# Two spacer tiles of 72 and 0 floats in place of 56 and 16: the experts' rows and activations move up by 64 bytes

## The chip, the cores and the metric

One core of a Trainium2 chip runs the whole program. The metric is the device time in microseconds (us) of one execution; three executions of the kernel before are known, and one more was taken with the profiler.

## The reference

The input is `x` of 8 x 2496 x 256 floats. A Fourier layer comes first: an FFT along the sequence, a complex 256 x 256 matrix, a soft threshold, the inverse FFT. Its result, 19968 rows of 256, goes through a mixture of 8 experts, of which each row takes one:

```python
logits = x @ w_gate + modality_bias[modality_id]
e_idx = np.argmax(logits, axis=1)
...
for e in range(E):
    mask = e_idx == e
    h = np.maximum(x[mask] @ w1[e], 0.0)
    out[mask] = gate_w[mask, None] * (h @ w2[e])
```

`w1[e]` is 256 x 1024, `w2[e]` 1024 x 256, all float32.

## The kernel before

The first part (classes `Attn`, `Route` and `SplitWeights`) does the Fourier layer in eight batches, routes each batch's rows, scatters them by expert into a DRAM buffer `xs`, and writes the experts' weights, split into a high and a low part, to DRAM. It ends near 639 us. The second part (class `Experts`) is the one whose tiles the change moves.

`Experts.run` goes through 40 tiles, 38 of 512 rows and 2 of 256 rows, each of one expert. Two sets of weight tiles take turns, `i % 2`: `wb[0]` lies at the far end of SBUF, `wb[1]` is made last in `Experts.pools`. For a tile, `load_x` reads the rows, `prep` transposes them on VectorE, `sums` forms four block sums, and `parts` splits every block into a rounded part `xh` (ScalarE, L937) and a rest `xl` (GpSimd mostly, L938). Then there are two layers on TensorE, each in two groups `grp`:

- `layer1` (L958) makes seven products of six matmuls each. The weights `w` are the stationary operand, loaded by LDWEIGHTS; `xh` or `xl`, 256 columns, is the moving operand. ScalarE copies three of the products to `v1`, `v2`, `v3` (L972), VectorE adds them (L967), ScalarE makes the rounded activations `hh` (L963) and VectorE the rest `hl` (L964).
- `layer2` (L1020) takes `hh` or `hl` as the stationary operand and 256 columns of `w2` as the moving one. ScalarE multiplies by the gate weight (L1037), and GpSimd scatters the rows to the output (L1053).

`run` interleaves the two layers by a fixed string, one product of `layer1` (six matmuls) and half a block of `layer2` (six matmuls) in turn, so that TensorE sees x x x x x x y y y y y y and so on; five small tiles of 32 rows are put in between (`tiny`). No planner and no due time is at work on the engines in this part: the order of each engine is the order in which the code records it.

Where tiles lie in SBUF is set by the order in which `Experts.pools` opens its pools, each behind the one before:

```python
self.x = pool("mx", 2)
self.tr = pool("mtr", 1)
self.cp = pool("mc", 1)
...
pad("mq0", PADS[0])
self.xp = pool("mxs", 1)
self.s = pool("ms", 1)
self.h = [pool("mh0", 1), pool("mh1", 1)]
pad("mq1", PADS[1])
self.wb.append(self.sets(ctx, 1))
```

`pad` makes a pool with one tile of so many floats per partition, which nothing reads or writes, and nothing at all for 0. Every tile behind `mq0` is a multiple of 1024 bytes long per partition (1024 for `xh` and `xl`, 2048 for `v`, 8192 for `hh`, `hl`, `w2`, `w3`, 14336 for `w0`, `w1`), so all tiles of a pool share one residue of 1024 bytes; pieces of a tile lie at that residue or 512 behind it.

One place of the first part is of use below. `Attn.pivot` (L424) has `pv` as the moving operand, whose first half lies at residue 448, and a piece of the tile `z` as the stationary one. The pieces of successive `j` begin 480 bytes apart (three steps of 160), so their residues run through multiples of 32 while the shape of the matmul stays; in batch 5 the first half's piece lies at 512 for j = 8, at 448 for j = 10 and at 384 for j = 12.

Of the kernel before, what the change touches and what calls it, by code (L numbers as in the profile page):

```python
# [41 lines left out]
SLOTS = 5  # L42
MORE = 16
EARLY = (6 * SEQ - 8 * (TP - 1)) // TP + 1 - E
PADS = (56, 16)
W1 = 2 * 2 * 7 * 128
W2 = 2 * 4 * 256
RAW = (2, 4, 6, 8, 10)
# [748 lines left out]
class Experts:  # L797
# [13 lines left out]
    def pools(self, ctx):  # L811
# [10 lines left out]
                                pattern=[[-1, 128]], channel_multiplier=1)  # L822
# [6 lines that stand above are left out]
# [750 lines left out]
```

## Time and profile before

| | |
|---|---|
| runs of the kernel before | 1508.08, 1508.33, 1509.77 us; median 1508.33 |
| the profiled execution | 1507.88 us, of which its span 1506.1 us |
| TensorE busy | 1430.0 us, 95% of the span |
| VectorE, ScalarE, GpSimd busy | 976.8, 799.9 and 804.7 us (65%, 53%, 53%) |
| mean granted TensorE clock | 0.982 |
| experts' matmuls | 7032, from 638.9 to 1493.8 us |

The span goes from the first to the last instruction of the profiled execution, and the 1.8 us that its time has over it lie around it. "Busy" is the time in which an engine has an instruction in work; matmuls overlap, so a TensorE that is busy all the time may still take longer or shorter steps from one matmul to the next. That step is read from the starts in the timeline.

### The profile page before, as it was taken

To read this page: it belongs to the slowest core of one execution; us is meant where nothing else is said; L and a number is where in the kernel's file an instruction comes from. 1 tells how busy PE (TensorE), PEld (TensorE's weight loads), DVE (VectorE), ACT (ScalarE), POOL (GpSimd) and SP (SyncE) were. 2 spreads that over 40 slices of the span, in tenths; PEclk is the share of its full clock that TensorE was granted. 3 is DMA by queue.
4 is the path that set the end of the run, shared out by engine and by line. 5 is a ranking of instruction groups with operands and counts; after the bars stand their busy time and mean duration, and the time that the engine had idled before them with its cause. 6 is when DMAs were issued, how large, how long until landed. Compare 5 with 4: busy or idle time off the path is not lost. (4 is left out here: it accounts for less than half of the span.)

```text
span 1506.1 us, 33730 instructions
## 1 busy us (share of the span) xinstructions
PE 1430.0 (95%) x11988; PEld 1366.3 (91%) x11988; DVE 976.8 (65%) x1882; ACT 799.9 (53%) x1715; POOL 804.7 (53%) x946
## 2 busy tenths in 40 slices
PE   8899898989898968989999999999999999999996
PEld 5789898979897968989999999999999999999995
DVE  4577776767686867577776566566656656665651
ACT  3456565656565434655455555555555555555542
POOL 2464767676767576734446844344434444444442
PEclk9999999999999989999999999999999999999998
DMA  8978787888787666851222359324212851582192
GB/s 269 284 231 255 241 273 243 273 247 268 251 268 232 220 206 197 297 175 36 54 57 60 98 149 360 78 50 102 70 36 51 285 187 42 166 305 55 40 353 75
DMA packets 222325, 268.85 MB, mean 179 GB/s; under 512 B 120784, under 2 KB 173771, under 8 KB 216901
## 3 DMA queue, kind: packets, MB, share of 16 engines
q1 hardware_dynamic: 202611, 223.67, 48.6%
q0 software_dynamic: 19408, 42.83, 8.9%
q8 instruction: 97, 1.59, 0.5%
q14 instruction: 79, 0.65, 0.1%
q10 hardware_dynamic: 130, 0.12, 0.0%
HBM read 326.99 MB, written 113.36 MB: 292 GB/s over the span
## 5 line engine op out<-in xcount | busy, mean ns | idle before, releaser
L1020 PE MATMUL y<-w,hh 128*128 128x256 f32 x2496 | 460.5, 279 | 0.0
L1020 PEld LDWEIGHTS y<-w,hh 128*128 128x128 f32 x2496 | 380.6, 189 | 3.7 <-issue 3.7
L1020 PE MATMUL y<-w,hl 128*128 128x256 f32 x1248 | 347.4, 278 | 2.2 <-DVE hl L964 2.0
L958 PE MATMUL X<-xh,w 128*128 128x256 f32 x1248 | 272.6, 282 | 6.9 <-ACT v L972 6.6
L1053 POOL DMA_INDIRECT out<-o,ix x156 | 154.9, 993 | 194.2 <-ACT o L1037 159.6
L1020 PEld LDWEIGHTS y<-w,hl 128*128 128x128 f32 x1248 | 234.2, 188 | 3.8 <-DVE hl L964 3.8
L958 PEld LDWEIGHTS X<-xh,w 128*128 128x128 f32 x1248 | 212.9, 188 | 12.4 <-ACT v L972 10.4
L938 POOL TENSOR_TENSOR xl<-tr,xh 128x256 fp32r<-128x256 f32 x118 | 88.4, 750 | 177.7 <-ACT xh L937 177.1
L964 DVE SCALAR_TENSOR_TENSOR hl<-Y,hh 128x512 fp32r<-128x512 f32 x156 | 107.8, 691 | 109.9 <-ACT hh L963 109.9
L958 PE MATMUL X<-xl,w 128*128 128x256 f32 x624 | 174.7, 280 | 1.1 <-POOL xl L938 1.1
L963 ACT ACTIVATE hh<-Y 128x512 fp32r<-128x512 f32 x156 | 93.3, 598 | 131.4 <-DVE Y L967 125.2
L424 PE MATMUL pv<-pv,z 128*120 128x136 f32 x704 | 118.8, 299 | 36.2 <-DVE z L414 35.3
L938 POOL TENSOR_TENSOR xl<-xt,xh 128x256 fp32r<-128x256 f32 x150 | 110.2, 746 | 79.9 <-ACT xh L937 75.0
L972 ACT COPY v<-X 128x512 f32<-128x512 f32 x228 | 133.6, 586 | 18.5 <-PE X L958 10.8
L424 PEld LDWEIGHTS pv<-pv,z 128*120 128x120 f32 x704 | 104.0, 200 | 39.1 <-issue 36.3
L958 PE MATMUL Z<-xh,w 128*128 128x256 f32 x608 | 132.3, 282 | 0.0
L382 PE MATMUL mx<-wmix,Xh 128*128 128x256 f32 x640 | 116.6, 305 | 6.6 <-DVE mx L372 5.6
L958 PEld LDWEIGHTS X<-xl,w 128*128 128x128 f32 x624 | 117.2, 188 | 1.6 <-POOL xl L938 1.6
L598 POOL DMA_INDIRECT xs<-x1b,si x88 | 89.5, 1017 | 49.5 <-DVE pl L430 21.2
L598 POOL DMA_INDIRECT xs<-x,si x88 | 89.4, 1016 | 42.4 <-issue 16.0
L967 DVE TENSOR_TENSOR Y<-Z,v 128x512 f32<-128x512 f32 x76 | 53.0, 698 | 88.8 <-ACT v L972 88.7
L429 ACT CAST ph<-pv 120x264 fp32r<-120x264 f32 x176 | 66.9, 381 | 80.5 <-PE pv L424 70.6
(259 smaller groups left out, 3484.0 us busy)
## 6 DMA issues: line engine op xcount, KB each, us to landing
w<-wsp SPq DMA_DIRECT2D x80, 1792.0 KB
w<-wsp SPq DMA_DIRECT2D x80, 1024.0 KB
a<-scr SPq DMA_DIRECT2D x160, 128.0 KB
x<-in_x SPq DMA_DIRECT2D x38, 512.0 KB
xt<-xs SPq DMA_DIRECT2D x152, 128.0 KB
scr<-ev SPq DMA_DIRECT2D x35, 480.0 KB
wsp<-wh SPq DMA_DIRECT2D x64, 256.0 KB
x<-in_moe_w SPq DMA_DIRECT2D x40, 256.0 KB
```

The costliest lines, as they stand in the source:

```text
L382: nc.tensor.matmul(mx[:, i, :], t[:, c, 1 - i, :], self.w[:, i, c, lo, :], start=False, stop=n == 5, skip_group_check=True)
L424: nc.tensor.matmul(ps[:PK, c * 128:c * 128 + D // 2 + E], self.z[:, o:o + 3, :, :].rearrange("p n k r -> p (n k r)"), self.pv[:, c, :], st ...
L429: nc.scalar.copy(ph, ps[:PK, :GC])
L598: i = self.nc.gpsimd.indirect_dma_start(out=self.xs, out_offset=bass.IndirectOffsetOnAxis(ap=si[:, k:k + 1], axis=0), in_=rows, in_offset= ...
L938: (nc.gpsimd if i or j in (0, 1, 6) else nc.vector).tensor_sub(sq(xl), v, sq(xh))
L958: nc.tensor.matmul(ps[:, u, :], w1[:, lo, u, blk, :], x, start=start and u == k == 0, stop=k == 2, skip_group_check=True)
L963: nc.scalar.activation(hh[:, par::2, o], v, AF.Relu)
L964: nc.vector.scalar_tensor_tensor(hl[:, par::2, o], v, 0.0, hh[:, par::2, o], ALU.max, ALU.subtract)
L967: nc.vector.tensor_add(out, a, b)
L972: nc.scalar.copy(v, ps)
L1020: nc.tensor.matmul(ps, h[:, q, o], w2[:, lo, q, :], start=grp == s % 2 == q == k == 0, stop=grp == 1 and q == 3 and k == 2, skip_group_che ...
L1053: ins = self.nc.gpsimd.indirect_dma_start(out=self.out, out_offset=bass.IndirectOffsetOnAxis(ap=ix, axis=0), in_=o, in_offset=None, bounds ...
```

## The change

```diff
-PADS = (56, 16)
+PADS = (72, 0)
```

`mq0` grows from 224 to 288 bytes per partition, and `mq1` (64 bytes) is no longer made. Every instruction of the built program stays, in the same order on all five engines and with the same waits. Of all tiles in SBUF, PSUM and DRAM only those of `mxs`, `ms`, `mh0` and `mh1` get other addresses, 64 bytes higher. By the built program's table of tiles, bytes within a partition and their residue of 1024:

```
tiles                     before            after
tr (mtr)                  61088,  672       61088,  672
xh0 .. xl6 (mxs)          69536,  928       69600,  992
v1, v2, v3 (ms)           83872,  928       83936,  992
hh, hl of group 0 (mh0)   90016,  928       90080,  992
hh, hl of group 1 (mh1)  106400,  928      106464,  992
w0 .. w3, set 1 (mw1)    122848,  992      122848,  992
w0 .. w3, set 0 (mw0)    184288,  992      184288,  992
```

So while TensorE streams `xh` and loads the next piece of `w` beside it, the two lay 64 bytes apart by residue (or 64 and 512), with the moving operand below; in the second layer, with `w2` moving and `hh` loaded, 64 apart with the moving one above. After the change both distances are 0 (or 512). At the seams between the layers, where `w2` streams and `w` is loaded, or `xh` streams and `hh` is loaded, the distance was 0 (or 512) before and stays so.

## Rows read from the trace of the kernel before

**Rows 1.** The page: busy time, share of the span, instructions of each engine.

```profile
PE 1430.0 (95%) x11988; PEld 1366.3 (91%) x11988; DVE 976.8 (65%) x1882; ACT 799.9 (53%) x1715; POOL 804.7 (53%) x946
```

**Rows 2.** Stretches: length, busy (instructions) of each engine, clock, DMA share, GB/s.

```profile
850.00:900.00 50.00, 50.00 (x432) 50.00 (x432) 30.55 (x50) 28.58 (x62) 28.96 (x37) 1.00 0.46 117
...
1000.00:1100.00 100.00, 100.00 (x872) 98.39 (x871) 61.01 (x96) 56.59 (x123) 45.01 (x59) 1.00 0.30 73
...
1300.00:1400.00 100.00, 100.00 (x867) 97.86 (x866) 60.36 (x95) 56.00 (x122) 46.01 (x62) 1.00 0.61 190
```

**Rows 3.** Waits of TensorE's weight loads, 850 to 1390 us: total us, times, longest.

```profile
PEld y L1020 <- issue: 3.3, 8, 0.4
PEld X L958 <- ACT hh L963: 1.6, 4, 0.4
```

**Rows 4.** Groups of instructions: the experts' matmuls; busy us, mean ns of one | idle before.

```profile
L1020 PE MATMUL y<-w,hh 128*128 128x256 f32 x2496 | 460.5, 279 | 0.0
L1020 PE MATMUL y<-w,hl 128*128 128x256 f32 x1248 | 347.4, 278 | 2.2 <-DVE hl L964 2.0
L958 PE MATMUL X<-xh,w 128*128 128x256 f32 x1248 | 272.6, 282 | 6.9 <-ACT v L972 6.6
L958 PE MATMUL X<-xl,w 128*128 128x256 f32 x624 | 174.7, 280 | 1.1 <-POOL xl L938 1.1
L958 PE MATMUL Z<-xh,w 128*128 128x256 f32 x608 | 132.3, 282 | 0.0
L958 PE MATMUL Z<-xl,w 128*128 128x256 f32 x304 | 85.1, 280 | 0.0
L958 PE MATMUL Y<-xh,w 128*128 128x256 f32 x336 | 73.0, 281 | 0.0
L958 PE MATMUL Y<-xl,w 128*128 128x256 f32 x168 | 47.1, 280 | 0.0
```

**Rows 5.** Timeline of PE, 1160.33 to 1164.55 us: start us, us, what.

```profile
1160.33 0.28 PE L958 MATMUL X<-xh,w 128*128 128x256 f32 x1
...
1160.92 0.28 PE L958 MATMUL X<-xh,w 128*128 128x256 f32 x1
1161.05 0.40 PE L1020 MATMUL y<-w,hh 128*128 128x256 f32 x2
...
1161.75 0.28 PE L958 MATMUL Y<-xh,w 128*128 128x256 f32 x1
...
1162.33 0.28 PE L958 MATMUL Y<-xh,w 128*128 128x256 f32 x1
1162.44 0.39 PE L1020 MATMUL y<-w,hh 128*128 128x256 f32 x2
...
1163.13 0.28 PE L958 MATMUL X<-xh,w 128*128 128x256 f32 x1
...
1164.55 0.28 PE L958 MATMUL Z<-xh,w 128*128 128x256 f32 x1
```

**Rows 6.** Timeline of PE, batch 5, j = 5, 8, 10, 12 and 21 of the pivot.

```profile
477.56 0.63 PE L424 MATMUL pv<-pv,z 128*120 128x136 f32 x4
...
480.06 0.63 PE L424 MATMUL pv<-pv,z 128*120 128x136 f32 x4
...
482.41 0.63 PE L424 MATMUL pv<-pv,z 128*120 128x136 f32 x4
...
484.78 0.63 PE L424 MATMUL pv<-pv,z 128*120 128x136 f32 x4
...
493.31 0.63 PE L424 MATMUL pv<-pv,z 128*120 128x136 f32 x4
```

**Rows 7.** Groups of instructions: those of the other engines that touch moved tiles.

```profile
L938 POOL TENSOR_TENSOR xl<-xt,xh 128x256 fp32r<-128x256 f32 x150 | 110.2, 746 | 79.9 <-ACT xh L937 75.0 <-PE Z L958 3.3
L964 DVE SCALAR_TENSOR_TENSOR hl<-Y,hh 128x512 fp32r<-128x512 f32 x156 | 107.8, 691 | 109.9 <-ACT hh L963 109.9
L963 ACT ACTIVATE hh<-Y 128x512 fp32r<-128x512 f32 x156 | 93.3, 598 | 131.4 <-DVE Y L967 125.2 <-PE Y L958 6.2
```

**Rows 8.** The chain that ended last: start us, us, what.

```profile
1497.60 0.98 POOL out L1053
```

## The prediction

> **What bounds the kernel now.** I read the page first, then a table of stretches, then the waits, and last the timeline of TensorE. On the page TensorE is busy for 95% of the span, the other engines for 53 to 65% [rows 1]. The change touches no tile that is used before the experts begin, so only the part from 639 us on matters. In that part's steady stretch TensorE is busy all the time: 50.00 of 50.00 us, 100.00 of 100.00 us, at a granted clock of 1.00, the higher of the two levels, 2.4 GHz [rows 2]. VectorE is busy for about 61 of 100 us, ScalarE for 56, GpSimd for 45 [rows 2]. In the 540 us from 850 to 1390 the largest waits of TensorE's weight loads come to 3.3 us in 8 times and 1.6 us in 4 times [rows 3]. So nothing but TensorE's own step, from the start of one matmul to the start of the next, sets the length of the stage. The end hangs on it too: the last scatter starts at 1497.60 us [rows 8], some 4 us behind the last of the experts' matmuls.
>
> That step is not one number. In the timeline, a group of six `layer1` and six `layer2` matmuls takes from 1160.33 to 1161.75, so 1.42 us; the next takes to 1163.13, so 1.38 us; the one after that to 1164.55, so 1.42 us again [rows 5]. Per matmul that is 118 ns and 115 ns. The shapes are the same, the clock is full, and no wait stands between. Slow and fast groups alternate. The two kinds of group have the same distances between their operands' addresses, so the distance alone doesn't choose the pace before the change.
>
> **The change, part by part.** It removes no instruction, adds none and reorders none; the queues of the DMAs, SP's and GpSimd's among them, are passed by nothing. No wait is added. What is left is five sets of instructions whose addresses move by 64 bytes.
>
> (1) TensorE. The experts' matmuls are 2496 + 1248 in the second layer and 1248 + 624 + 608 + 304 + 336 + 168 = 3288 in the first, 7032 together [rows 4], each with a weight load. That makes 7032 / 12 = 586 groups of twelve, 293 of them slow and 293 fast if they alternate throughout. The trace shows no expert matmul with other addresses, so the cost per matmul is bounded, not read. From below: all groups could come out fast, 293 x (1.42 - 1.38) = 11.7 us less [rows 5]. From above: all could come out slow, 11.7 us more. Between these I take zero, from the row in which the distance does vary. In the pivot of batch 5, the piece of `z` for j = 8 lies 64 bytes above `pv` by residue (the first layer's distance before the change), for j = 10 at the same residue (the distance after it), for j = 12 64 bytes below (the second layer's before). The four records take 0.63 us in all three [rows 6], and the same in each of the 17 pivots from j = 5 to j = 21, whose residues run through other multiples of 32 (the first and the last of them stand there too). Those distances hold for one of the three steps within a row and move with it in the others. The last digit is 10 ns over three steps, so this excludes a stall of more than some 3 ns per step. It doesn't exclude the 3 ns between the two paces, and it is a matmul of 136 columns and not 256: hence the bounds stay.
>
> Beside these rows stands a rule of the Trainium skill, page "SBUF — State Buffer", section "Who interferes with whom": TensorE has two independent read ports, one for the moving operand and one for weight loads, and never waits on anyone. By that rule the change is worth exactly 0. The two paces of 1.42 and 1.38 us [rows 5] are not contradicted by it, but the rule gives no reason for them either, so I don't let it close the bounds.
>
> (2) Other engines. ScalarE writes `hh` in 598 ns, VectorE reads it and writes `hl` in 691 ns, GpSimd reads `xh` and writes `xl` in 746 ns [rows 7]; 64 bytes of address may shift these. If each took 1% longer, that is 6 to 8 ns apiece. It lies beside TensorE's work, with 39 to 55 us of 100 free on each engine [rows 2], and costs nothing. Without that cover, as in the first tile, where TensorE waited 6.6 us for `v` [rows 4], 1% is 0.07 us.
>
> (3) The pools. One pool fewer and a larger spacer issue nothing: 0.
>
> The sum is 0. Against the profiled execution that gives 1506.1 + 1.8 = 1507.9 us; the median of the three runs shown is 0.45 us higher, and I give the forecast on the median's footing: 1508.3 us. A measurement of this kernel can tell about 0.2%, 3.0 us, from no change.
>
> **The rivals.** *Faster: one residue keeps the fast pace.* The pace changes where one layer's matmuls give way to the other's, and there the distance between the two reads jumps before the change: 0 at the seam, 64 below in `layer1`, 64 above in `layer2`. After it there is no jump. If the jump is what throws the fast pace over, groups stay at 1.38 us, and the time falls by up to 11.7 us, to 1496.6 [rows 5]. For it speaks that the pace switches from one group to the next, at a seam, and that the fast group's last `layer1` step, at distance 0, is short: 1162.33 to 1162.44, 0.11 us [rows 5]. Against it: inside a group the distance jumps as well, and there the pace holds. The slow group's halves take 0.72 and 0.70 us, the fast group's 0.69 and 0.69 [rows 5].
>
> *Slower: one residue keeps or makes the slow pace.* Two streams that start in the same place collide on every step, not only on the two seam steps of twelve. In the slow group the last `layer1` step, the one that already has distance 0, is the longest: 1160.92 to 1161.05, 0.13 us, against 118 ns on the mean [rows 5]. If distance 0 brings this about everywhere, fast groups become slow ones: up to 11.7 us more, 1520.0 us. It decides from the point at which more than 3.0 / 0.04 = 75 of the 293 fast groups are lost. Against it stands the 0.11 us at the same distance in the fast group, and the pivot.
>
> A sentence of the same skill bears on both rivals, page "TensorE: Matmul & The Clock Gate", section "LDWEIGHTS (loading the stationary operand)": a weight load takes its columns divided by 1.2 GHz, by which 128 columns come to an estimate of 107 ns. By it a load is about as long as the 256-column matmul beside it, so a slip on either side shows in the step; the trace's steps of 115 and 118 ns lie a little above.
>
> *That the change doesn't do what it says* can be left out: the table of tiles shows the new addresses.
>
> **How the numbers follow.** The forecast of no change gets 0.43: the pivot's rows and the mixed record of the seams are for it. Slower gets 0.31 and faster 0.26: each has one seam step for it and one against it, and the longest step that the stage shows stands at distance 0. The rivals' full prices are 1496.6 and 1520.0 us; each is reached only if every group changes, so I cut the outermost 1.5 to 2 us and give 1498 to 1518 us. The forecast's own range is 1505.3 to 1511.3.
>
> **What would show it right or wrong.** Right: twelve-matmul groups alternate between 1.42 and 1.38 us after the change as well, a steady 100 us still holds 867 to 872 matmuls [rows 2], and the first expert matmul still starts at 639 us. Faster: groups of 1.38 us follow one another, and 1.4% more matmuls (1.40 / 1.38) stand in 100 us. Slower: 1.42 us or more throughout, and 1.4% fewer. A gain or loss ahead of 639 us, or waits of TensorE on ScalarE, VectorE or GpSimd of more than the 3.3 us shown [rows 3], would prove the reasoning wrong, whatever the total.

## The result, and the profile after

The changed kernel took 1530.36 us (median of 4 runs, 1529.01 to 1531.98) beside 1509.05 us for the kernel before (4 runs, 1508.08 to 1509.94): a ratio of 1.0142, 95% interval 1.0124 to 1.0159. It is slower by 1.4%, where no change was forecast and 1518 us was the upper end of the range. The profiled execution took 1531.98 us with a span of 1530.2 us, 24.1 us more than the span before.

The page of the kernel after (busy time, share of the span, instructions of each engine) answers to [rows 1]:

```profile
PE 1454.9 (95%) x11988; PEld 1392.4 (91%) x11988; DVE 977.0 (64%) x1882; ACT 801.6 (52%) x1715; POOL 805.3 (53%) x946
```

Only TensorE's busy time has moved, from 1430.0 to 1454.9 us. The other engines' stays within 2 us. The same stretches as in [rows 2], for the kernel after (length, busy and instructions of each engine, clock, DMA share, GB/s):

```profile
850.00:900.00 50.00, 50.00 (x419) 50.00 (x419) 29.31 (x47) 27.53 (x59) 28.59 (x35) 1.00 0.37 102
...
1300.00:1400.00 100.00, 100.00 (x842) 97.85 (x842) 58.86 (x93) 54.02 (x117) 45.19 (x59) 1.00 0.60 187
```

TensorE is still busy all the time at a granted clock of 1.00, but 50 us hold 419 matmuls in place of 432, and 100 us hold 842 in place of 867: 3% fewer. No wait explains it. The waits of the weight loads from 850 to 1390 us, for the kernel after, are those of [rows 3] to the digit:

```profile
PEld y L1020 <- issue: 3.3, 8, 0.4
PEld X L958 <- ACT hh L963: 1.6, 4, 0.4
```

The groups of the experts' matmuls in the kernel after (busy us, mean ns of one | idle before) answer to [rows 4], those of the other engines to [rows 7]; `PEld` are the weight loads:

```profile
L1020 PE MATMUL y<-w,hh 128*128 128x256 f32 x2496 | 473.7, 283 | 0.0
L1020 PE MATMUL y<-w,hl 128*128 128x256 f32 x1248 | 353.8, 283 | 1.4 <-DVE hl L964 1.1
L958 PE MATMUL X<-xh,w 128*128 128x256 f32 x1248 | 277.9, 285 | 6.3 <-ACT v L972 6.1
...
L1020 PEld LDWEIGHTS y<-w,hl 128*128 128x128 f32 x1248 | 239.4, 192 | 2.7 <-DVE hl L964 2.7
L958 PEld LDWEIGHTS X<-xh,w 128*128 128x128 f32 x1248 | 216.7, 192 | 10.5 <-ACT v L972 8.5
...
L958 PE MATMUL Z<-xh,w 128*128 128x256 f32 x608 | 134.8, 284 | 0.0
...
L938 POOL TENSOR_TENSOR xl<-xt,xh 128x256 fp32r<-128x256 f32 x150 | 110.3, 747 | 80.3 <-ACT xh L937 73.7
L964 DVE SCALAR_TENSOR_TENSOR hl<-Y,hh 128x512 fp32r<-128x512 f32 x156 | 107.9, 691 | 110.3 <-ACT hh L963 110.3
L963 ACT ACTIVATE hh<-Y 128x512 fp32r<-128x512 f32 x156 | 93.3, 598 | 142.2 <-DVE Y L967 135.8
```

The two groups of weight loads in the kernel before:

```profile
L1020 PEld LDWEIGHTS y<-w,hl 128*128 128x128 f32 x1248 | 234.2, 188 | 3.8 <-DVE hl L964 3.8
L958 PEld LDWEIGHTS X<-xh,w 128*128 128x128 f32 x1248 | 212.9, 188 | 12.4 <-ACT v L972 10.4
```

The records of the matmuls are 2 to 5 ns longer on the mean (283 in place of 279 or 278, 285 and 284 in place of 282), those of the loads 4 ns (192 in place of 188). ScalarE and VectorE take 598 and 691 ns as before, and GpSimd's `xl` 747 in place of 746. Then the step itself, in the timeline of PE of the kernel after (start us, us, what), which answers to [rows 5]:

```profile
1160.99 0.28 PE L958 MATMUL X<-xh,w 128*128 128x256 f32 x1
1161.11 0.28 PE L958 MATMUL X<-xl,w 128*128 128x256 f32 x1
...
1161.71 0.40 PE L1020 MATMUL y<-w,hh 128*128 128x256 f32 x2
...
1162.43 0.28 PE L958 MATMUL Z<-xh,w 128*128 128x256 f32 x1
...
1163.15 0.40 PE L1020 MATMUL y<-w,hh 128*128 128x256 f32 x2
...
1163.87 0.28 PE L958 MATMUL X<-xh,w 128*128 128x256 f32 x1
```

Six `layer1` steps take from 1160.99 to 1161.71, 0.72 us; six `layer2` steps take to 1162.43, 0.72 us again; and so on: 1.44 us for each twelve, 120 ns for each step. The alternation between 1.42 and 1.38 us [rows 5] is gone, and what came in its place is a third pace, slower than either. The end follows TensorE as before [rows 8]: the last scatter starts 4.1 us behind the last expert matmul (1517.60 us), by the timeline of GpSimd at

```profile
1521.68 0.98 POOL L1053 DMA_INDIRECT out<-o,ix  x1 [0.30 <-issue]
```

**Where the time went.** I took the starts of all 7032 expert matmuls from both traces. The stage from the first of these to the last lasts from 638.9 to 1493.5 us before (854.6) and from 640.9 to 1517.6 us after (876.7): 22.1 of the 24.1 us. The other 2 us lie ahead of the stage, where the two programs are the same: over all the profiled executions of this study the stage begins between 636.8 and 643.1 us, so that is spread between executions. Within the stage I set aside the steps of 130 ns or more, in which TensorE waits or has another instruction in between. The mean of the others is 116.29 ns before (6915 steps) and 119.93 ns after (6927), and 6655 of the latter are 120 ns to the nanosecond. 7031 x 3.64 ns = 25.6 us. The longer steps gave 3.5 us of this back: over the pace, they hold 36.95 us before and 33.44 us after. Most of it is at the weight loads, whose waits for `v` and `hl` fell from 10.4 and 3.8 us to 8.5 and 2.7: a later TensorE waits less for the other engines. 25.6 - 3.5 = 22.1 us.

### The profile page after: what moved, and what is told of

Read it like the earlier page. It is cut to its first block, busy times and chain, and to the rows that moved or that the text cites. A ratio compares the mean times of both kernels' runs of the same rounds, so it can differ in the third digit from the quotient of the medians.

```text
span 1530.2 us, 33730 instructions
## 1 busy us (share of the span) xinstructions
PE 1454.9 (95%) x11988; PEld 1392.4 (91%) x11988; DVE 977.0 (64%) x1882; ACT 801.6 (52%) x1715; POOL 805.3 (53%) x946
## 5 line engine op out<-in xcount | busy, mean ns | idle before, releaser
L1020 PE MATMUL y<-w,hh 128*128 128x256 f32 x2496 | 473.7, 283 | 0.0
L1020 PEld LDWEIGHTS y<-w,hh 128*128 128x128 f32 x2496 | 389.1, 192 | 3.7 <-issue 3.7
L1020 PE MATMUL y<-w,hl 128*128 128x256 f32 x1248 | 353.8, 283 | 1.4 <-DVE hl L964 1.1
L958 PE MATMUL X<-xh,w 128*128 128x256 f32 x1248 | 277.9, 285 | 6.3 <-ACT v L972 6.1
L1020 PEld LDWEIGHTS y<-w,hl 128*128 128x128 f32 x1248 | 239.4, 192 | 2.7 <-DVE hl L964 2.7
L958 PEld LDWEIGHTS X<-xh,w 128*128 128x128 f32 x1248 | 216.7, 192 | 10.5 <-ACT v L972 8.5
L598 POOL DMA_INDIRECT xs<-x,si x88 | 89.2, 1014 | 44.0 <-issue 18.6
```

Source lines behind the costliest of these rows:

```text
L598: i = self.nc.gpsimd.indirect_dma_start(out=self.xs, out_offset=bass.IndirectOffsetOnAxis(ap=si[:, k:k + 1], axis=0), in_=rows, in_offset= ...
L958: nc.tensor.matmul(ps[:, u, :], w1[:, lo, u, blk, :], x, start=start and u == k == 0, stop=k == 2, skip_group_check=True)
L1020: nc.tensor.matmul(ps, h[:, q, o], w2[:, lo, q, :], start=grp == s % 2 == q == k == 0, stop=grp == 1 and q == 3 and k == 2, skip_group_che ...
```

## The experiments

All vary only where tiles lie; no instruction is added, removed or reordered, and nothing is left out of the computation. I call the **distance** of a step, from the start of one matmul to the start of the next, the residue of its moving operand minus that of the piece being loaded beside it, the one that the next matmul uses. Four distances describe a kernel: in `layer1`, in `layer2`, at the seam from `layer1` to `layer2` and at the seam back. The kernel before has -64, +64, 0, 0; after the change it is 0, 0, 0, 0. The letters of the theories are defined within each expectation. Mean steps are worked out as above. "Beside" is the kernel before on the same chip in the same session. Kernels have one run, without an interval, unless a ratio is given. Fifteen runs of the kernel before in the last session lie between 1503.69 and 1514.06 us, so what differs by less than some 10 us is told apart by the mean step, not by a single time.

The edits need pads in other places: `mq1` ahead of the pools `mh0`, `mh1`, a new `mq2` behind them, in some a gap between `w1` and `w2` of each weight set, and in some one ahead of `wb[0]` at the far end. Each diff below shows only its values; they go in like this (`PADS[0]` stays with `mq0`; a value of 0 makes no tile; added lines move the line numbers by up to 5):

```diff
-        self.h = [pool("mh0", 1), pool("mh1", 1)]
         pad("mq1", PADS[1])
+        self.h = [pool("mh0", 1), pool("mh1", 1)]
+        pad("mq2", PADS[2])
...
+        p.tile([128, GAP], F32, name=f"wgap_{i}")
...
+        ctx.enter_context(tc.tile_pool(name="mq3", bufs=1, side="right")).tile([128, RIGHT], F32, name="mq3t")
```

| kernel | layer1, layer2, seams | mean step, ns | us | beside |
|---|---|---|---|---|
| before | -64, +64, 0, 0 | 116.29 | 1509.05 | |
| after | 0, 0, 0, 0 | 119.93 | 1530.36 | 1509.05 |
| e1_all928 | 0, 0, 0, 0 | 119.93 | 1529.91 | 1509.32 |
| f1_all960 | 0, 0, 0, 0 | 119.92 | 1530.38 | 1507.55 |
| e2_256 | +256, -256, 0, 0 | 119.93 | 1531.81 | 1509.32 |
| e3_rows0 | 0, +64, +64, 0 | 116.58 | 1511.57 | 1509.32 |
| e4_acts0 | -64, 0, -64, 0 | 116.95 | 1512.86 | 1509.32 |
| e5_moving_above64 | +64 in all | 117.75 | 1515.88 | 1508.77 |
| e8_moving_below64 | -64 in all | 116.42 | 1509.43 | 1508.77 |
| e6_128 | -128, +128, 0, 0 | 118.47 | 1521.80 | 1508.77 |
| e7_32 | -32, +32, 0, 0 | 117.50 | 1512.42 | 1508.77 |
| e9_above32 | +32 in all | 117.28 | 1514.71 | 1504.61 |
| e10_above96 | +96 in all | 119.97 | 1536.72 | 1504.61 |
| e11_below96 | -96 in all | 118.29 | 1520.67 | 1504.61 |
| e12_below32 | -32 in all | 118.33 | 1522.00 | 1504.61 |
| f3_flip | +64, -64, 0, 0 | 116.37 | 1509.61 | 1507.55 |
| f2_noseam | -64, +64, +64, -64 | 113.68 | 1495.39 | 1507.55 |
| f5_noseam_timed (the same) | -64, +64, +64, -64 | 113.65 | 1496.88 | 1508.38 |
| f4_noseam2 | -64, +64, -64, +64 | 116.29 | 1509.17 | 1507.55 |
| f6_seam128 | -64, +64, +128, -128 | 117.68 | 1517.27 | 1508.38 |

### Is it the place or the distance?

Two kernels put all tiles at one residue that is not 992, and one moves the rows and activations on by 256 bytes.

```diff
-PADS = (56, 16)
+PADS = (56, 0, 0)      # e1_all928: all at 928
+RIGHT = 16
...
+PADS = (64, 0, 0)      # f1_all960: all at 960
+RIGHT = 8
...
+PADS = (136, 0, 192)   # e2_256: x, h at 224, weights at 992
```

> All four kinds of tiles at residue 928: rows, activations as in the kernel before, both weight sets 64 bytes lower, so the distance between the moving operand and the piece being loaded is 0 everywhere, at another place than in the changed kernel. Theory 1 (the distance sets the pace: two reads that begin at one residue collide): every step 120 ns as in the changed kernel, about 1530 us. Rival theory 2 (the place of rows and activations, residue 992, is the bad one): steps alternate between about 118 and 114 ns as before, about 1509 us.

> Distance 0 at every step once more, with all tiles at residue 960, which begins a stretch of 64 bytes, where 928 and 992 lie in the middle of one. If the distance sets the pace: 120 ns at every step, about 1530 us, as at 928 and 992. If it is the place within 64 bytes together with the distance: another pace, 1489 to 1518 us.

> Rows and activations 256 bytes above the weights by residue (224 against 992). Theory 1: no step of 120 ns in a row; 1509 us or less, and 1494 us if the fast pace of 113 to 115 ns then holds throughout. Theory 2: rows and activations are away from 992, so the pattern of the kernel before, about 1509 us.

Measured: 1529.91, 1530.38 and 1531.81 us, mean steps of 119.93, 119.92 and 119.93 ns, uniform as after the change. In e1_all928 `xh` and `hh` are where the kernel before has them, and the weights have moved. Its timeline of PE shows the 1.44 us per twelve, and the stretch of 1300 to 1400 us 843 matmuls:

```profile
1160.34 0.28 PE L959 MATMUL Z<-xh,w 128*128 128x256 f32 x1
...
1161.78 0.28 PE L959 MATMUL X<-xh,w 128*128 128x256 f32 x1
...
1300.00:1400.00 100.00, 100.00 (x843) 97.85 (x842) 58.29 (x92) 53.26 (x116) 43.48 (x58) 1.00 0.59 184
```

So the address of the rows and activations by itself is not the cause. A distance of 0 in all steps makes them 120 ns long whatever the place (928, 960 or 992). A distance of 256 bytes counts as 0, which neither theory of e2_256 had expected.

### Which layer pays?

```diff
-PADS = (56, 16)
+PADS = (72, 240, 16)   # e3_rows0: x at 992, h at 928
...
+PADS = (56, 16, 0)     # e4_acts0: x at 928, h at 992
```

> Rows at 992 (distance 0 to w in the first layer), activations at 928 (64 below w2, as before). Theory 1: the first layer's 3288 matmuls step by 120 ns, the second layer's 3744 do not; about 1518 us (half of the loss), if the pace doesn't carry over from one layer to the other. Theory 2: the same share for the rows at 992. A third reading, that the lock needs distance 0 at every step and the jumps at the seams: alternating groups, about 1509 us.

> Rows at 928 (64 below w, as before), activations at 992 (distance 0 to w2). Theory 1: the second layer's 3744 matmuls step by 120 ns, the first layer's do not; about 1520 us. Theory 2: the same. The third reading (the lock needs distance 0 at every step): alternating groups, about 1509 us.

Measured for e3_rows0: 1511.57 us. The timeline of PE shows the two layers apart:

```profile
1161.28 0.28 PE L959 MATMUL X<-xh,w 128*128 128x256 f32 x1
1161.40 0.39 PE L1021 MATMUL y<-w,hh 128*128 128x256 f32 x2
...
1161.97 0.28 PE L1021 MATMUL y<-w,hl 128*128 128x256 f32 x1
1162.08 0.28 PE L959 MATMUL Z<-xh,w 128*128 128x256 f32 x1
...
1162.80 0.39 PE L1021 MATMUL y<-w,hh 128*128 128x256 f32 x2
```

From the first `layer2` matmul to the first of `layer1` it is 0.68 us, 113 ns a step; from there to the next `layer2` matmul 0.72 us, 120 ns a step. Over the stage the means are 113.72 and 119.82 ns. The layer put at distance 0 pays the 120 ns, and the other, right behind it, does not: the cost stays with the steps of one layer and does not spread. The 1518 us of theory 1 were missed because the other layer ran at 113.7 ns, faster than in the kernel before.

The steps at the seams don't fit my definition of the distance, though. The step from `layer1` to `layer2` is at +64 and takes 0.12 us (1161.28 to 1161.40; 120.64 ns on the mean of 541), the step back is at 0 and takes 0.11 us (1161.97 to 1162.08; 113.66 ns on the mean of 500). In the kernel before, too, the steps at the seams, at distance 0, take 116.44 and 114.88 ns on the mean, not 120. If the distance is taken to the piece that the matmul itself uses, loaded one step earlier, e3_rows0 has six steps at 0 and six at +64 and fits. No run was made to tell the two ways of counting apart.

In e4_acts0 (1512.86 us, where theory 1 expected about 1520) the parting is less clean: `layer1` at -64 has 115.82 ns, `layer2` at 0 has 117.95, in a fixed pattern in which six successive steps take 119, 112, 117, 118, 120 and 121 ns. Its `layer2` is slower than its `layer1`, but not at 120 throughout; steps at one distance differ with their place in the twelve.

### Is any distance but 0 good, if it never changes?

Here the distance is one and the same in both layers and at both seams: no jump, and no step at 0. All have the moving tiles at 992; `GAP` goes into both weight sets.

```diff
-PADS = (56, 16)
+PADS = (72, 240, 0)    # e5_moving_above64, GAP = 16
...
+PADS = (72, 16, 0)     # e8_moving_below64, GAP = 240
...
+PADS = (72, 248, 0)    # e9_above32, GAP = 8
...
+PADS = (72, 232, 0)    # e10_above96, GAP = 24
...
+PADS = (72, 24, 0)     # e11_below96, GAP = 232
...
+PADS = (72, 8, 0)      # e12_below32, GAP = 248
```

> Every moving operand (rows, w2, w3) at 992, every loaded one (w0, w1, activations) at 928: the distance is 64 bytes at every step, the seams between the layers included, and never 0. Theory 1 (the distance between the two reads of one step sets its pace; a step at distance 0 costs 120 ns and, at a seam, also throws the pace of the next steps over): all steps 113 to 114 ns, 7032 x (116.3 - 113.4) ns = 20 us less than the kernel before, about 1489 us. Rival (the alternation of the kernel before has another cause, not the seams at distance 0): layer 1 or layer 2 groups still alternate, 1505 to 1512 us.

> The same with the sign turned: every moving operand 64 bytes below the loaded one by residue (992 against 32). Theory 1: as the run before, about 1489 us, if the sign makes no difference; if a moving read that starts below the loaded one runs into it later, steps above 114 ns and more than 1495 us.

> Every moving operand 32 bytes above the loaded one, at every step. If the collision reaches over 64 bytes, 120 ns throughout and about 1531 us; if 32 bytes part the reads, 113 to 118 ns, 1489 to 1516 us.

> Every moving operand 96 bytes above the loaded one, at every step, seams included. Theory 1 (one distance, one pace, no lock away from 0): a pace that is the same all through, below 120 ns. If the two reads are parted best near the middle of the 256-byte period, 113 to 114 ns and about 1489 us; if 64 above (117.75 ns, 1515.9 us) is typical of all distances but 0, about 1515 us.

> Every moving operand 96 bytes below the loaded one, at every step. With 64 below, steps held at 113.4 or at 118 ns and switched only where TensorE was interrupted (1509 us). If 96 below leaves only the faster of the two, about 1489 us; if both, 1500 to 1515 us; if only the slower, about 1518 us.

> Every moving operand 32 bytes below the loaded one, at every step. If the collision reaches over 64 bytes, 120 ns throughout and about 1531 us; if 32 bytes part the reads, 113 to 118 ns, 1489 to 1516 us, perhaps with two paces as at 64 below.

Measured: at +64, 1515.88 us in three rounds, a ratio of 1.0053 (1.0036 to 1.0070) to the kernel before, at a nearly uniform 117.75 ns. At -64, 1509.43 us. At +32, -32, +96 and -96, 1514.71, 1522.00, 1536.72 and 1520.67 us, beside 1504.61. None beats the kernel before, and +96 is as slow as 0: 119.97 ns, here in steps of 115 to 125. So "0 is bad, anything else is good", by which e5 and e8 were expected at about 1489 us, is false; +96 and -32 came out slower than anything that their expectations had for a distance off 0.

The kernel at -64 shows something else. Two stretches of its timeline of PE, of the same tiles and the same distances:

```profile
866.75 0.28 PE L960 MATMUL X<-xh,w 128*128 128x256 f32 x1
...
868.11 0.28 PE L960 MATMUL Y<-xh,w 128*128 128x256 f32 x1
...
1160.62 0.28 PE L960 MATMUL Y<-xh,w 128*128 128x256 f32 x1
...
1162.03 0.28 PE L960 MATMUL X<-xh,w 128*128 128x256 f32 x1
```

A twelve takes 1.360 us in the first and 1.413 us in the second, 113.4 and 118 ns per step. Around each the pace holds for long: every twelve without an interruption from 880 to 950 us takes 1.413 us. It changes only where at least one step of over 200 ns lies between, from 950 us on mostly at the small tiles. The same addresses thus allow two paces; what chooses between them at such a place wasn't found.

### Smaller and larger distances in the layers, with seams at 0

```diff
-PADS = (56, 16)
+PADS = (64, 0, 8)      # e7_32: x, h at 960
...
+PADS = (40, 0, 32)     # e6_128: x, h at 864
...
+PADS = (88, 0, 240)    # f3_flip: x, h at 32
```

> Rows and activations both 32 bytes below the weights by residue. If the reads collide within a stretch of 64 bytes, 120 ns at every step, about 1530 us; if 32 bytes are enough to part them, alternating groups as before, 1500 to 1512 us.

> Rows and activations both 128 bytes below the weights by residue. If distances repeat every 128 bytes, this is distance 0 again: 120 ns at every step, about 1530 us. If they repeat every 256 bytes, it is another distance, with the seams at 0: alternating groups as before, 1500 to 1512 us.

> The mirror image of the kernel before: rows 64 above w, w2 64 below the activations, seams at distance 0. If only the size of the distance counts: alternating groups, about 1509 us. If 64 above is the slower sign in the first layer too, as in the run with 64 above everywhere: steps of 117.75 ns in the first layer and 113.4 or 118 in the second, 1500 to 1516 us.

Measured: 1512.42 us (117.50 ns), 1521.80 us (118.47 ns, successive steps from 112 to 123 ns) and 1509.61 us (116.37 ns). With the signs exchanged, f3_flip has the mean step of the kernel before within 0.1 ns, but not its alternation: its twelves take 1.401 and 1.392 us in turn, with `layer1` the slower layer in one and `layer2` in the next, where the kernel before has 1.420 and 1.373. For e6_128 neither expectation held, neither 120 ns at every step nor 1500 to 1512 us. The mean at 32 lies between 64 and 0, but that at 128 is no lower than at 32, so there is no plain falling of the cost with the distance.

### Are the seams the cause of the alternation?

The last idea: in the kernel before, the two steps of distance 0 in each twelve, at the seams, are what keeps throwing the fast pace over. These kernels keep the -64 and +64 of the layers and take the seams off 0, by setting `w2` apart from `w` and `hh` apart from `xh`.

```diff
-PADS = (56, 16)
+PADS = (56, 240, 32)   # f2_noseam, f5_noseam_timed: GAP = 240
+RIGHT = 16
...
+PADS = (40, 16, 0)     # f4_noseam2: GAP = 16
...
+PADS = (56, 224, 48)   # f6_seam128: GAP = 224
+RIGHT = 32
```

> The layers keep the distances of the kernel before (rows 64 below w, w2 64 above the activations), but the seams are no longer at 0: from layer 2 to layer 1 64 below, from layer 1 to layer 2 64 above. If the seam at distance 0 is what switches the pace in the kernel before: the pace holds from group to group and changes only where TensorE is interrupted by a small tile, 1489 to 1515 us. If the change of sign between the layers switches it: alternating groups, about 1509 us.

> The same kernel as the one before with the seams off zero (distance -64 in layer1, +64 in layer2 as in the kernel before, +64 and -64 at the two seams instead of 0), timed. Theory A (a seam at distance 0 costs by itself and throws the next group into the slow pace; without one nothing starts it): 113.7 ns per matmul throughout as in the single look, 7032 x (113.7 - 116.3) = 18 us less in the profiled stretch, of which disturbed steps keep some; 1494 to 1498 us, a ratio of 0.990 to 0.994 to the kernel before. Theory B (the start of an execution chooses the pace, and the single look was a lucky one): executions spread between 1495 and 1509 us, median above 1500.

> The layers at the distances of the kernel before, the seams at 64 too but with the signs exchanged: from layer 2 to layer 1 64 above, from layer 1 to layer 2 64 below. Expected as of the run with the other signs: no alternation from group to group if the seam at distance 0 is its cause, 1489 to 1515 us; alternation and about 1509 us if not.

> Layers as in the kernel before (-64 in layer1, +64 in layer2), seams at +128 and -128 instead of 0. Theory A (any seam off 0 keeps the fast pace): 113 to 114 ns per matmul, 1494 to 1498 us. Theory C (the steps of +64 and -64 at the seams are what keeps it, and 128 behaves like the run with +128 and -128 inside the layers, whose steps were 112 to 123 ns): a fixed pattern within every twelve with a mean of 115 to 119 ns, 1503 to 1524 us.

Measured: with seams at +64 and -64 the kernel is **faster than both**, 1495.39 us in its first run, and 1496.88 us (6 runs, 1493.33 to 1498.36) beside 1508.38, a ratio of 0.9921 (0.9899 to 0.9942). The timeline of PE and the stretch of 1300 to 1400 us of f5_noseam_timed show the fast pace, which 368 of 369 twelves without an interruption have:

```profile
1161.48 0.28 PE L963 MATMUL X<-xh,w 128*128 128x256 f32 x1
...
1162.84 0.28 PE L963 MATMUL Z<-xh,w 128*128 128x256 f32 x1
...
1300.00:1400.00 100.00, 100.00 (x883) 97.75 (x883) 61.00 (x95) 56.28 (x123) 43.45 (x58) 1.00 0.54 174
```

A twelve takes 1.36 us, and 100 us hold 883 matmuls where [rows 2] has 867. The mean step is 113.65 ns. 7031 x 2.640 = 18.56 us were to be had; the stage, from 638.6 to 1481.2 us, is 12.03 us shorter. The rest went into new waits, of which the groups of the same kernel show a part:

```profile
L963 PE MATMUL X<-xh,w 128*128 128x256 f32 x1248 | 269.4, 281 | 8.5 <-ACT v L977 8.4
...
L963 PE MATMUL Z<-xh,w 128*128 128x256 f32 x608 | 129.1, 278 | 1.4 <-DVE Y L972 1.4
```

Idle time ahead of `X` is 8.5 us in place of 6.9, and ahead of `Z` 1.4 in place of 0.0 [rows 4]: a TensorE that is ahead of before waits for ScalarE's `v` and VectorE's `Y` at the places where those are only just done. Other waits are too short to be listed there, but the step behind them is long: 49 steps to an `X<-xl` of some 220 ns, in place of 26, which is 2.6 us; all 23 more stand behind a weight load of `X<-xh` that waited for `v`. At 982.94 us, for one, the weight load of `X<-xh` waits 49 ns for `v`, and the step behind it takes 223 ns. In all, the steps of 130 ns and more hold 43.49 us over the pace in place of 36.95, which is the missing 6.5 us.

But the other two kernels don't fit the idea. f4_noseam2 has the seams at -64 and +64 with the signs exchanged, f6_seam128 has them at +128 and -128; no step of either is at 0, and they take 1509.17 us (116.29 ns: 114.62 in `layer1`, 117.77 in `layer2`) and 1517.27 us (six runs, a ratio of 1.0056, 1.0038 to 1.0074; 117.68 ns), as theory C had it. So the seams matter, but taking them off 0 isn't enough. Nor does the order of the distances decide: f2_noseam and f4_noseam2 both have six steps at -64 and six at +64 in a twelve, only begun one step apart, and differ by 2.6 ns on the mean. What f2_noseam has and these don't is that `xh` and `w2`, the two moving operands, lie at one residue, and so every load of `w` meets -64 and every load of `hh` +64. In e3_rows0, where `xh` and `w2` share a residue and loads of `hh` meet +64 alone too, the steps within `layer2` have the fast 113.7 ns, though not the one at the seam to it (120.64). This is an observation and no rule: e5 and e8, whose moving operands lie at one residue as well, don't hold the fast pace throughout.

## Why the prediction was wrong

**What bounds the kernel: right.** Nothing but TensorE's own step sets the length of the stage. The waits of the weight loads in the steady stretch are unchanged, and the stage's 22.1 us are a longer step less 3.5 us that other waits gave back.

**Term (1): wrong, and it is the step that failed.** "Between these I take zero, from the row in which the distance does vary" was a conclusion from the pivot to the experts. The pivot's matmul is one of 136 columns, the experts' one of 256, and the text said so and took the zero all the same. At equal residues the 256-column step is 120 ns in place of the mean of 116.29, in four kernels at four sets of addresses (after, e1, f1, e2) and in the one layer of e3_rows0 that has distance 0. The reading of the pivot stands: to the nanosecond, the last two steps of the records for j = 8, 10 and 12 are 115 ns each, at whatever distance. It doesn't carry over to the experts, and why not wasn't tried.

The bound from above failed with it. "All could come out slow, 11.7 us more" took the slower of two paces seen for the slowest that there is. There was a third: 1.44 us per twelve, which at 586 twelves is 586 x 1.44 - 293 x (1.42 + 1.38) = 23.4 us more. The row that hinted at it had been read: the last `layer1` step of the slow twelve, 1160.92 to 1161.05, was 0.13 us, longer than its pace [rows 5], and its distance was the one that the change was going to make everywhere. To the timeline's 10 ns it is at least 0.12 us, and priced from that step, not from the group around it, the upper bound is 7032 x 0.12 - 820.4 = 23.4 us or more. That this lies so near the 25.6 us is in part luck: to the nanosecond the step is 120 ns, but the one behind it, at +64, is 121, and in the fast group the same distance has 113. The row could widen the bound; it couldn't forecast the time.

**Terms (2) and (3): right.** 598, 691 and 747 ns on the three other engines in place of 598, 691 and 746 [rows 7]; nothing from the pools. One reading in (2) is off, without weight for the sum: the 6.6 us of waits for `v` are ten waits from 643 to 800 us, of which 4.5 us lie in the first 20 us.

**The slower rival had the cause, with its price too low.** Two streams that start at the same place throughout do cost on every step; e1, f1 and e2 show that this holds at other places too, and e3 that one layer alone can pay it. What makes them slow each other down no run shows. The term was sized as 0.04 us for each of 293 twelves; it measured 12 x 3.64 ns = 0.044 us for each of all 586. The 0.11 us at the same distance in the fast group was held against the rival; in e4_acts0, too, a step's length varies with its place (112 to 121 ns in a layer at distance 0), so one step at a seam doesn't give the price of a run of such steps.

**The faster rival fell, though a part of what it saw is there.** Without the jumps at the seams the alternation did end, in the kernel after and in e5_moving_above64. But the one pace left was a slow one each time. And f5_noseam_timed keeps the fast pace with a jump from -64 to +64 at every seam. It is not the jump by itself that throws the pace over.

**The two rules of the Trainium skill.** By the Trainium skill, page "SBUF — State Buffer", section "Who interferes with whom", TensorE's two read ports make it wait on nobody, and the change would be worth 0. The trace disagrees for the two streams of TensorE itself: 119.93 ns against 116.29 with nothing but 64 bytes of address between. Between engines no run here tests that section; between the two ports themselves its word "independent" doesn't hold for the time. The estimate of 107 ns for a load from the Trainium skill, page "TensorE: Matmul & The Clock Gate", section "LDWEIGHTS (loading the stationary operand)", lies below every pace seen (113.4, 118 and 120 ns). The loads' own records, which overlap the matmuls, take 188 ns before and 192 after; no run shows whether the load or the matmul carries the difference.

**What would show it.** The signs named for slower (1.42 us or more throughout, 1.4% fewer matmuls) came, at 1.44 us and 3%. The signs for right reasoning on the rest came too: the stage begins at 640.9 us, within the spread of 636.8 to 643.1, and TensorE's waits are the 3.3 us shown.

**What stays open.** Which rule sets the pace at distances other than 0 and 256. -64 and +64 allow 113.4 ns but don't secure it (e5: 117.75; e8: both); +96 is as slow as 0; -32 and +32 differ (118.33 and 117.28), as do -96 and +96; f2 and f4 differ with the same distances in the same order; and the seams of e3 fit only if the distance is counted another way. No theory of mine gives the right number for all of these kernels.

## What to carry to other kernels

Where 128x256 matmuls follow one another back to back and nothing waits, look at the step from start to start, not at the busy time: a kernel "100% busy" here ran at anything from 113.7 to 120 ns per matmul, by the addresses of its tiles alone. Equal residues of the moving and the loaded operand (modulo 256 bytes) were slow in all four kernels that had them throughout; spacer tiles add no instruction, and one arrangement found so was 0.8% faster than the kernel before. And when a cost is bounded by two levels that the trace shows, a single step outside both can be a third level and belongs into the bound; a matmul of another shape isn't a stand-in for it.

## What the runs showed of the hardware that was not expected

- At a granted clock of 1.00 the step of a 128x256 fp32r matmul with its weight load has at least three levels that can hold for many steps, 113.4, 118 and 120 ns, and they depend on where the two operands lie in a partition. At 2.4 GHz these are 272, 283 and 288 cycles.
- The relevant distance repeats after 256 bytes as far as one run shows (e2_256 against the kernel after: 119.93 ns both).
- At distance -64 throughout (e8_moving_below64) one program holds either of two paces, 1.360 or 1.413 us per twelve, for tens of us, and changes over only where a step of over 200 ns lies between.
- Less time per matmul isn't all kept: f5_noseam_timed lost 6.5 of 18.6 us to waits, most of them for ScalarE and VectorE at places where these were just in time before, and the kernel after got 3.5 of 25.6 us back, most of it in the same kind of place.
